# Fetching the global query and key rows of a windowed attention by indirect gathers, and giving batch 1 the schedule of the later batches

## The chip, the cores and the metric

The kernel runs on one core of a Trainium2 chip. Its engines are TensorE (PE, with its weight loads shown apart as PEld), VectorE (DVE), ScalarE (ACT), GpSimd (POOL) and SyncE (SP, which only issues transfers). Sixteen DMA engines move data between the chip's memory and the core. The metric is device time in microseconds (us) for one execution, the median of several; lower is better.

## The reference

A windowed attention with global tokens is followed by a two-layer block with a sine activation. B = 8 batches, H = 8 heads, S = 576 positions, D = 64, and NG = 8 positions in `global_idx`, the same for all batches and heads.

```python
scores = scale * np.matmul(q, k.transpose(0, 1, 3, 2))
mask = np.abs(pos[:, None] - pos[None, :]) <= 32
mask = mask | is_global[:, None] | is_global[None, :]
attn = softmax(np.where(mask, scores, -1e9))
x = matmul(attn, v)            # to (B*S, H*D) = (4608, 512)
h = x @ w_in                   # 512 -> 2048
g = h + sin(alpha * h)**2 / alpha
out = g @ w_out                # 2048 -> 512, float32
```

So every position sees its neighbours within 32 and the eight global positions, and the eight global positions see everything.

## The kernel before, in words

**Layout.** Positions go in 12 blocks of 48. A block's keys are 112 neighbours (48 and 32 on each side) and 8 global keys, so 120 rows; its queries are its own 48 and the 8 global ones, 56 columns. `kTw[hp]` (hp is one of four pairs of heads) holds the transposed keys of the blocks, with the global keys in columns 112 to 119 (`KB` to `KB + NG`); `qT[hp]` holds the transposed queries with the global ones in columns 48 to 55. Both are overwritten for each batch. Eight blocks make a unit, six units a batch. For a unit, `stage_Q` computes scores (PE), their exponential (ACT) and a product with a 0/1 mask (DVE, L474); `stage_D` the sums by a matmul with ones and a reciprocal as exp(-ln) on ACT; `stage_V` the product with the values in `VW` (batch parity) and a scaling on DVE into `xT`. `stage_G` finishes the global queries with eight small POOL copies into `xT` (L549).

**Phases.** Phase 0 is attention of batch 0. Then come, nine times, `mm1(p)`, 16 slots of `x @ w_in` with the activation, and, from phase 1 on, attention of batch p with `mm2(p - 1)`, the product with `w_out`, as filling between its stages. The first slots of `mm2` need the first half of `w_out`, the later ones the second. Attention of batch p + 1 has its first two head pairs transposed inside `mm1(p)` (`stage_T`, L430). From batch 2 on, all batches run the same list of steps, a `step(j)` in `attention`, with counts of filling slots after each (L816). Phases 0 and 1 have orders of their own, written out by hand (L782 and L794), in which K, q stand for transposes of keys and queries, G (or k, p) for the one-hot products below, Q, D, V for the stages, F for a slot of filling.

**Global rows before.** Batches 0 and 1: `globals_hp` (L369) multiplies the key and query tiles with a one-hot matrix `OH` on PE, 12 matmuls each for keys and queries of a head pair, and ACT or DVE copy the result into `kTw` and `qT` (L382). In phase 0 this is done within the order, in phase 1 for two head pairs within `mm1(0)` and for two in the order of phase 1. Batches 2 to 7: SP reads the eight indices into registers and issues transfers with register offsets (L339, L345): eight of batch 0's values, then eight each for values, keys and queries of all batches, 64 rows of 256 bytes each. They land in a part of the second `H2b` buffer. Near the end of phase 1 DVE casts the keys and queries (L354), PE transposes them in eight matmuls (L360), DVE copies them to `GT` (L365), and POOL copies from `GT` into `kTw` and `qT`, two copies for each head pair (`globals_in`, L396 and L400), in the batch before they are needed.

**Masks before.** Units 0 to 2 of batch 0 are masked on DVE as elsewhere. In units 3 to 5 PE adds a bias instead: two matmuls (L457) put a large negative `BIAS` in the scores first.

**Queues.** POOL issues all loads that cast from float32 to bfloat16: keys and queries of batch 0 in four pairs of heads (L131), its values (L114, L115, L118), the shifted second copy of `VW` (L146, L147), both halves of `w_in`, the values, keys and queries of batch 1, then the first half of `w_out`; the eight copies of L549 follow, then the second half of `w_out` (L710), in this order. POOL's queue, like each engine's, is in order. POOL transfers use eight semaphores in turn, so each waits until the eighth before it has landed. SP issues the gathers, the shift of `VW` for later batches and the output.

Of the kernel before, what the change touches and what calls it, by code (L numbers as in the profile page):

```python
# [13 lines left out]
DT = mybir.dt  # L14
# [3 lines left out]
def kernel(  # L18
# [61 lines left out]
    GT = const.tile([P, 2, NHP, B, NG], BF, name="GT")  # L80
# [3 lines left out]
    gN = [  # L84
        H2[1][0 : NG * B, 2 * i : 2 * i + 2, :].rearrange("p a n -> p (a n)").bitcast(F32)
        for i in range(3)
    ]
    gB = [H2[1][0 : NG * B, 6 + i, :] for i in range(2)]
    OH = const.tile([P, NTW, NG], BF, name="OH")
# [61 lines left out]
    def global_v(b):  # L151
# [27 lines left out]
    T6 = setup.tile([P, NTW], F32, name="T6")  # L179
    nc.gpsimd.iota(  # L180
        T6[:], pattern=[[TW, NTW]], base=0, channel_multiplier=1,
        allow_small_or_imprecise_dtypes=True,
    )
    kq0 = kq_loads(0, PAIRS)
    v0 = v_loads(0, ((0, H),))
    for f in kq0[:4]:
        f()
# [14 lines left out]
    zero_v(0)  # L202
# [3 lines left out]
    for f in v0 + kq0[4:]:  # L206
        f()
    Kps0 = psA0.tile([P, 2 * CH], BF, name="o2")

    def edges(t_):  # L210
# [5 lines left out]
    Vg32 = setup.tile([P, DM], F32, name="Vg32")  # L216
    zero(Vg32[96:128])
# [15 lines left out]
    Gf = setup.tile([P, NG], F32, name="Gf")  # L233
    nc.vector.tensor_copy(out=Gf[:], in_=gall[:].bitcast(DT.int32)[:, 0::2])
    nc.vector.tensor_tensor(
        out=OH[:], in0=T6[:, :, None].to_broadcast([P, NTW, NG]),
        in1=Gf[:, None, :].to_broadcast([P, NTW, NG]), op=ALU.is_equal,
# [38 lines left out]
    BIAS = setup.tile([P, NW + NB // 2, QC], BF, name="BIAS")  # L276
# [29 lines left out]
    def bias():  # L306
        nc.vector.tensor_scalar(
            out=BIAS[:], in0=MASK[:], scalar1=1.0, scalar2=-NEG, op0=ALU.subtract, op1=ALU.mult
        )

# [10 lines left out]
    VgZ = VgX[96:128, :, 0, :]  # L321

    def globals_v0():
        nc.vector.tensor_copy(out=VgZ, in_=Vg32[96:128].rearrange("p (h d) -> p h d", d=D))

    def globals_vn():
        G = VgX[0 : NG * B]
        nc.scalar.copy(out=G[:, :, 0, :], in_=gN[2].rearrange("p (h d) -> p h d", d=D))
        nc.scalar.copy(
            out=G[:, :, 1:, :], in_=G[:, :, 0:1, :].to_broadcast([NG * B, H, NU - 1, D])  # L330
        )

    def gather_all():
# [4 lines left out]
        for j in range(NG):  # L338
            nc.sync.dma_start(  # L339
                out=Vg32[KB + j : KB + j + 1, :].rearrange("p (h d) -> p h d", d=D),  # L340
                in_=v[0, :, bass.ds(regs[j], 1), :].rearrange("h o d -> o h d"),
            )

        def gather(i, src, j):
            nc.sync.dma_start(  # L345
                out=gN[i][j : NG * B : NG, :].rearrange("b (h d) -> b h d", d=D),
                in_=src[:, :, bass.ds(regs[j], 1), :].rearrange("b h o d -> b h (o d)"),
            )

        return [partial(gather, i, src, j) for i, src in ((2, v), (0, k), (1, q)) for j in range(NG)]  # L350

    def globals_cast():
        for i in range(2):
            nc.vector.tensor_copy(out=gB[i], in_=gN[i])  # L354

    def globals_all(pool, tag):
        gps = pool.tile([P, 2, NHP, NG * B], BF, name=tag)
        for i in range(2):
            for hp in range(NHP):
                nc.tensor.transpose(  # L360
                    out=gps[:, i, hp, :],
                    in_=gB[i][:, hp * P : (hp + 1) * P],
                    identity=identb[0 : NG * B, 0 : NG * B],
                )
        nc.vector.tensor_copy(  # L365
            out=GT[:].rearrange("p i h b g -> p i h (b g)"), in_=gps[:]
        )

    def globals_hp(b, hp, pool, tag, copy=nc.vector.tensor_copy, which=(0, 1)):  # L369
        gp = pool.tile([P, 2, NG], F32, name=tag)  # L370
        for i in which:
            src = qk[b][1 - i]
            for j in range(NTW):
                for t, pr in heads:
                    nc.tensor.matmul(
                        out=gp[pr, i, :],
                        lhsT=src[:, 2 * hp + t, j, :], rhs=OH[0:TW, j, :],
                        start=(j == 0), stop=(j == NTW - 1), skip_group_check=True,
                    )
        for i in which:  # L380
            dst = (kTw[hp][:, :, KB : KB + NG], qT[hp][:, :, QB:QC])[i]
            copy(  # L382
                out=dst, in_=gp[:, i, None, :].to_broadcast([P, NW, NG])
            )
# [10 lines left out]
    def globals_in(b, hp, eng=nc.gpsimd):  # L395
        eng.tensor_copy(  # L396
            out=kTw[hp][:, :, KB : KB + NG],
            in_=GT[:, 0, hp, b, None, :].to_broadcast([P, NW, NG]),
        )
        eng.tensor_copy(  # L400
            out=qT[hp][:, :, QB:QC],
            in_=GT[:, 1, hp, b, None, :].to_broadcast([P, NW, NG]),
# [27 lines left out]
    def stage_T(b, hp, pool, tag):  # L430
        T_K(b, hp, Kps, nc.vector.tensor_copy)
        T_Q(b, hp, pool, tag, nc.scalar.copy)
        if b == 1:
            globals_hp(b, hp, psC, "ops", nc.scalar.copy)
# [16 lines left out]
    def stage_Q(psA, b, n):  # L451
        Sp = psA.tile([P, 2, CH], F32, name="Sp")
        i0 = blocks(n)[0][1]
        biased = b == 0 and n >= NUN - NBIAS
        if biased:
            for t, pr in heads:
                nc.tensor.matmul(  # L457
# [13 lines left out]
        if biased:  # L471
            return E
# [275 lines left out]
    def start_sync():  # L748
        gathers.extend(gather_all())
        for f in gathers:  # L750
            f()
# [125 lines left out]
```

## Time and profile before

| What | Value |
|---|---|
| median of 10 runs | 380.0 us (376.95 to 383.35) |
| the profiled execution's own time | 381.6 us |
| its span, first to last instruction | 379.8 us |
| PE busy | 353.1 us, 93% of the span |
| ACT, DVE, POOL busy | 249.3, 233.6, 209.2 us |
| mean granted PE clock | 0.942 of full |
| phase 0 and `mm1(0)` | 0 to about 55.5 us |
| attention 1 with `mm2(0)` | 59.3 to 90.7 us |
| attention 2 with `mm2(1)` | 106.3 to 129.0 us |

The profile is of one execution, whose own time is 1.8 us above its span. A page gives the busy time of each engine, the span cut into 40 slices of 9.5 us with a digit for each engine's busy share in tenths, the clock that PE was granted in the same slices, the chain of work that ended last, and groups of instructions. A timeline lists instructions with start and duration, and in brackets how long the engine had been idle and what ended it. "Matmul busy" counts overlapping instructions, and small matmuls that follow one another are listed with a duration of about 0.2 us each although they start more closely.

### The profile page before, as it was taken

The page shows a single profiled execution, that of the slowest core. Times are in us where ns is not written, and L with a number is a line of the kernel's source. Part 1 is how long each engine was busy: PE and PEld are TensorE (multiplying, and loading weights), DVE is VectorE, ACT ScalarE, POOL GpSimd, SP SyncE. Part 2 cuts the span into 40 slices and gives each one's busy share as a digit, 9 for nine tenths or more (in the row PEclk, how much of TensorE's full clock was granted, in tenths as well). Part 3 has the DMA queues.
Part 4 walks back from the last instruction along what each step waited for, and adds up shares of the span by engine and source line. Part 5 has one row for each costly group of instructions (what it writes and reads, how often), then busy time and mean ns, then how long its engine had stood idle before and what let it go on. Part 6 is the DMA issues. An engine that isn't in the chain of part 4 may idle for free.

```text
span 379.8 us, 9614 instructions
## 1 busy us (share of the span) xinstructions
PE 353.1 (93%) x3832; PEld 175.9 (46%) x3832; DVE 233.6 (61%) x502; ACT 249.3 (66%) x381; POOL 209.2 (55%) x300
## 2 busy tenths in 40 slices
PE   6689986989999999999999999999999999999996
PEld 5444443444444444444544454444444444444444
DVE  6534583454876488648864886388638863866520
ACT  4547673465887588858885888588858884845411
POOL 9863496014893389338943894389438302965100
PEclk9555895799999999999999999999999999999999
DMA  9999999913199329942994279427933011000112
GB/s 80 167 196 173 188 173 165 99 57 100 35 65 179 110 41 58 176 109 49 58 173 113 51 52 168 115 59 50 173 101 71 2 42 73 0 2 28 55 58 83
DMA packets 132919, 35.55 MB, mean 94 GB/s; under 512 B 121674, under 2 KB 126698, under 8 KB 132874
## 3 DMA queue, kind: packets, MB, share of 16 engines
q0 software_dynamic: 121968, 19.91, 71.0%
q1 hardware_dynamic: 10602, 14.89, 14.0%
q8 instruction: 30, 0.49, 0.5%
q10 hardware_dynamic: 304, 0.14, 0.1%
q14 instruction: 15, 0.12, 0.1%
HBM read 38.95 MB, written 9.44 MB: 127 GB/s over the span
## 4 chain that ended last, share of the span: by engine, by line
PE 60%; ACT 14%; DVE 9%; DMA 6%; POOL 6%; issue 3%; POOLq 1%; ACTq 0%; DVEq 0%
PE hb L617 24%; PE ops L654 14%; PE o L654 11%; DMA w_out<-in_moe_w_out_dram 6%; ACT E L470 5%; PE num L515 3%; ACT Sb L624 3%; DVE kTw L417 2%; DVE S L632 2%; ACT L568 2%; PE Sp L464 2%; DVE H2b L607 2%; PE hb L654 2%; ACT rec L505 2%; ACT lnd L503 2%
## 5 line engine op out<-in xcount | busy, mean ns | idle before, releaser
L624 ACT ACTIVATE Sb<-hb,alphaT 128x512 bf16<-128x512 f32 x144 | 97.8, 686 | 57.3 <-PE hb L617 55.3
L617 PE MATMUL hb<-xT,w_in 128*128 128x512 bf16 x576 | 131.4, 382 | 1.3 <-DVE H2b L607 1.0
L632 POOL TENSOR_TENSOR S<-Sb 128x512 bf16<-128x512 bf16 x110 | 111.6, 1041 | 36.2 <-ACT Sb L624 36.2
L607 DVE SCALAR_TENSOR_TENSOR H2b<-S,recipT,hb 128x512 bf16<-128x512 bf16 x144 | 102.3, 740 | 25.7 <-POOL S L632 25.7
L617 PEld LDWEIGHTS <-w_in 128*128 128x128 bf16 x576 | 55.5, 98 | 69.0 <-issue 4.7
L654 PE MATMUL ops<-w_out,H2b 128*128 128x512 bf16 x304 | 76.9, 387 | 3.8 <-DMA w_out<-in_moe_w_out_dram 3.8
L654 PEld LDWEIGHTS <-H2b 128*128 128x128 bf16 x560 | 50.3, 99 | 62.1 <-issue 9.9
L470 ACT ACTIVATE E<-Sp 128x896 bf16<-128x896 f32 x48 | 43.5, 907 | 19.7 <-PE Sp L464 19.6
L654 PE MATMUL o<-w_out,H2b 128*128 128x512 bf16 x224 | 56.2, 390 | 0.0
L474 DVE TENSOR_TENSOR E<-E,MASK 128x896 bf16<-128x896 bf16 x45 | 28.3, 630 | 40.2 <-ACT E L470 40.2
L549 POOL COPY xT<-xg 128x4 bf16 x64 | 12.9, 201 | 61.0 <-DVE xg L547 57.4
L503 ACT ACTIVATE lnd<-den 128x384 f32<-128x384 f32 x48 | 23.5, 490 | 23.0 <-PE den L497 23.0
L533 DVE TENSOR_TENSOR xT<-num,rec 128x384 bf16<-128x384 f32 (+1 forms) x60 | 25.7, 449 | 12.5 <-PE num L515 9.8
L632 DVE TENSOR_TENSOR S<-Sb 128x512 bf16<-128x512 bf16 x26 | 18.2, 702 | 19.8 <-ACT Sb L624 19.6
L464 PE MATMUL Sp<-qT,kTw 64*128 64x56 bf16 x768 | 20.9, 192 | 8.5 <-ACT E L470 3.1
L464 PEld LDWEIGHTS <-kTw 64*128 64x128 bf16 x768 | 15.8, 97 | 23.9 <-issue 14.6
L515 PEld LDWEIGHTS <-VW 120*64 120x64 bf16 (+1 forms) x768 | 17.5, 117 | 19.3 <-issue 11.7
L505 ACT ACTIVATE rec<-lnd 128x384 f32<-128x384 f32 x48 | 25.1, 523 | 1.5
L417 DVE COPY kTw<-Kps 128x1344 bf16<-128x1344 bf16 x29 | 24.5, 846 | 1.0 <-PE Kps L408 1.0
L396 POOL COPY kTw<-GT 128x96 bf16<-128x96 bf16 x24 | 6.4, 269 | 32.6 <-PE num L515 20.5
L515 PE MATMUL num<-E,VW 120*64 120x56 bf16 (+1 forms) x720 | 20.4, 198 | 2.3 <-DVE gn L482 0.8
L131 POOL DMA_DIRECT2D KS<-in_k_dram x18 | 20.4, 1134 | 0.3 <-issue 0.3
(129 smaller groups left out, 305.5 us busy)
## 6 DMA issues: line engine op xcount, KB each, us to landing
out_dram<-osb SPq DMA_DIRECT2D x35, 256.0 KB
KS<-in_k_dram POOLq DMA_DIRECT2D x14, 288.0 KB, 8.3
QS<-in_q_dram POOLq DMA_DIRECT2D x14, 288.0 KB, 9.3
VW<-in_v_dram POOLq DMA_DIRECT2D x12, 336.0 KB, 11.2
VW<-VW SPq DMA_DIRECT2D x7, 384.0 KB
w_in<-in_moe_w_in_dram POOLq DMA_DIRECT2D x2, 1024.0 KB, 15.2
w_out<-in_moe_w_out_dram POOLq DMA_DIRECT2D x2, 1024.0 KB, 23.9
VW<-VW SPq DMA_DIRECT2D x7, 240.0 KB
```

The source lines that it names most:

```text
L417: copy(out=kTw[hp][:, :, 0:KB], in_=bass.AP(tensor=base.tensor, offset=base.offset, ap=[list(base.ap[0]), [QB, NW], [1, KB]],),)
L464: nc.tensor.matmul(out=Sp[:, t, m * QC : (m + 1) * QC], lhsT=kTw[hp][pr, i, :], rhs=qT[hp][pr, i, :], start=not biased, stop=True, skip_gr ...
L470: nc.scalar.activation(out=E[:], in_=Sp[:, :, 0:EW], func=AF.Exp, scale=scale)
L474: nc.vector.tensor_tensor(out=E[:], in0=E[:], in1=mk[:, None, :].to_broadcast([P, 2, EW]), op=ALU.mult)
L503: nc.scalar.activation(out=lnd[:], in_=den[:, :, 0:QB], func=AF.Ln)
L505: nc.scalar.activation(out=rec[:], in_=lnd[:], func=AF.Exp, scale=-1.0)
L515: nc.tensor.matmul(out=num[pr, m, :], lhsT=W[0:nk, i % 2, 2 * hp + t, i // 2, :], rhs=E[0:nk, t, m * QC : (m + 1) * QC], start=b > 0 or m ...
L607: nc.vector.scalar_tensor_tensor(out=H2b[:, n_, :], in0=s_[:], scalar=recipT[:, n_ : n_ + 1], in1=h_, op0=ALU.mult, op1=ALU.add,)
L617: nc.tensor.matmul(out=h2[:], lhsT=w_in[:, ci, nt * P : (nt + 1) * P], rhs=xT[:, ci, c * CH : (c + 1) * CH], start=(ci == 0), stop=(ci == ...
L624: nc.scalar.activation(out=Sb[:], in_=h2[:], func=AF.Sin, scale=alphaT[:, nt : nt + 1])
L632: eng.tensor_tensor(out=S2[:], in0=Sb[:], in1=Sb[:], op=ALU.mult)
L654: nc.tensor.matmul(out=ops[:], lhsT=H2b[:, nt, ts * P : (ts + 1) * P], rhs=w_out[:, nt, :], start=(nt == 0), stop=(nt == NT - 1),)
```

## The change

Four indirect transfers on POOL bring, for four batches at once, the global rows of all heads: `GKQ` has a row for each of (batch in the half, head pair, global index), 128 in all, for keys and queries and for the even and odd head of a pair. The row numbers `rowi` are computed on DVE from two small iotas and the indices. The first four are issued right after the first pair of key and query loads, so the rest of batch 0's loads stand behind them in POOL's queue; four more, for batches 4 to 7, are issued in phase 1 behind the loads of batch 2. `globals_t` transposes a half (four matmuls and one copy): the first half ("A") within phase 0, the second in phase 2. `globals_in` now serves all batches: for batch 0 on ACT and DVE (g0 to g3), for batch 1 on POOL (n0 to n3, in phase 0, behind the first half of `w_out` and ahead of the eight copies of `stage_G`).

With that go `globals_hp`, `OH`, the sixteen SP gathers of keys and queries and the eight of batch 0's values; batch 0's global values are taken from the gathered values of all batches by a small matmul with `SEL`. The bias matmuls go: units 3 to 5 of batch 0 get the DVE mask. Phase 1's own order goes: batch 1 runs the step list of the later batches. Cut to its core:

```diff
     kq0 = kq_loads(0, PAIRS)
     v0 = v_loads(0, ((0, H),))
-    for f in kq0[:4]:
+    for f in kq0[:2]:
         f()
...
+    rowi = const.tile([P, 1], DT.uint32, name="rowi")
+    nc.vector.scalar_tensor_tensor(
+        out=rowi[:], in0=I8[:, 0:1], scalar=float(2 * S), in1=Gsel[:, 0:1],
+        op0=ALU.mult, op1=ALU.add,
+    )
+    def gather_kq(i):
+        for kq, src in ((0, k), (1, q)):
+            for t in range(2):
+                nc.gpsimd.indirect_dma_start(
+                    out=GKQ[:, kq, i, t, :],
+                    out_offset=None,
+                    in_=src.rearrange("b h s d -> (b h s) d"),
+                    in_offset=bass.IndirectOffsetOnAxis(ap=rowi[:, 0:1], axis=0),
+                    element_offset=(i * 4 * H + t) * S * D,
+                )
+
     zero_v(0)
...
-    for f in v0 + kq0[4:]:
+    gather_kq(0)
+    for f in kq0[2:4] + v0 + kq0[4:]:
         f()
...
     def globals_v0():
-        nc.vector.tensor_copy(out=VgZ, in_=Vg32[96:128].rearrange("p (h d) -> p h d", d=D))
+        G = VgX[0 : NG * B]
+        nc.vector.tensor_copy(out=G[:, :, 0, :], in_=gN[:].rearrange("p (h d) -> p h d", d=D))
+        zp = psC.tile([P, DM], F32, name="ops")
+        nc.tensor.matmul(
+            out=zp[96:120, :], lhsT=SEL[:], rhs=G[0:NG, :, 0, :],
+            start=True, stop=True, skip_group_check=True,
+        )
+        nc.scalar.copy(out=VgX[96:120, :, 0, :], in_=zp[96:120, :].rearrange("p (h d) -> p h d", d=D))
...
+    def globals_t(i, pool, tag):
+        gps = pool.tile([P, 2, P], BF, name=tag)
+        for kq in range(2):
+            for t, pr in heads:
+                nc.tensor.transpose(out=gps[pr, kq, :], in_=GKQ[:, kq, i, t, :], identity=identb[:])
         nc.vector.tensor_copy(
-            out=GT[:].rearrange("p i h b g -> p i h (b g)"), in_=gps[:]
-        )
...
+            out=GT[:, :, i * B // 2 : (i + 1) * B // 2].rearrange("p i b h g -> p i (b h g)"), in_=gps[:]
+        )
...
-        if b == 1:
-            globals_hp(b, hp, psC, "ops", nc.scalar.copy)
...
-        biased = b == 0 and n >= NUN - NBIAS
-        if biased:
-            for t, pr in heads:
-                nc.tensor.matmul(
-                    out=Sp[:, t, 0:EW], lhsT=identb[:],
-                    rhs=BIAS[:, i0 : i0 + NB, :].rearrange("p u c -> p (u c)"),
-                    start=True, stop=False, skip_group_check=True,
-                )
...
-        go("warm sync K0 q0 G0 Q0 K1 k1 q1 p1 loads Q1 D0 Q2 D1 bias K2 k2 q2 p2 D2 Q3 K3 q3 D3 k3 p3 vg V0 Q4 V1 D4 Q5 V2 "
-           "V3 D5 V4 alpha V5 last keep vn wo")
...
-        go("L " * len(ld) + "F F Q0 Q1 K2 q2 G2 F F Q2 D0 K3 q3 G3 F D1 Q3 V0 F D2 Q4 V1 F F D3 Q5 gc V2 "
-           "F F D4 all V3 F D5 V4 F V5 g0 g1 g2 g3 last F F F F")
...
+        order = (
+            "warm K0 q0 A g0 Q0 K1 q1 g1 loads Q1 D0 Q2 D1 n0 n1 K2 q2 g2 D2 Q3 vg K3 q3 g3 D3 Q4 V0 V1 D4 Q5 n2 n3 V2 V3 D5 V4 "
+            "alpha V5 last keep vn wo"
+        )
...
+                parts, last = attention(p, psA, {2: -2, 3: 0})
+                counts = [1, 1, 1, 1, 1, 2, 2, 1, 0]
+                fill.pop(0)()
+                fill.pop(0)()
+                if p + 1 < B:
+                    with_extra(parts, load_slots(p + 1), 0, 4)
+                    if p == 1:
+                        parts[4] = partial(chain, parts[4], partial(gather_kq, 1))
+                    if p == 2:
+                        parts[4] = partial(chain, parts[4], partial(globals_t, 1, psA, "qp"))
```

## The prediction, made before the changed kernel was run

> **What bounds the kernel now.** I read the slices first, to find where PE is not the limit.
>
> ```profile
> PE   6689986989999999999999999999999999999996
> ...
> PEclk9555895799999999999999999999999999999999
> DMA  9999999913199329942994279427933011000112
> ```
>
> From slice 8 on (76 us) PE is busy nine tenths at full clock, and nothing in the change shortens that part. The first eight slices are different: the DMA engines are full, PE is not, and its clock is half for long. So the change is decided before 91 us. The windows, cut by phase, say what that front costs:
>
> ```profile
> core 0: us, PE busy (x) PEld busy (x) DVE busy (x) ACT busy (x) POOL busy (x), PEclk, DMA share, GB/s
> ...
> 59.20:71.00 11.80, 10.72 (x118) 5.28 (x120) 2.35 (x5) 2.83 (x4) 3.88 (x4) 0.50 2.17 158
> 71.00:90.70 19.70, 17.45 (x260) 8.90 (x257) 10.83 (x35) 11.89 (x20) 3.33 (x16) 1.00 0.35 57
> ...
> 106.30:129.70 23.40, 22.62 (x321) 11.15 (x320) 15.19 (x39) 16.93 (x27) 12.60 (x24) 1.00 1.37 117
> ```
>
> Attention 1 takes 31.4 us (59.3 to 90.7); attention 2, with the same stages and the same 16 filling slots, 23.4. Of the 8.0 us between them the first 11.8 run at clock 0.50. Then the chain that ended last, in order of time:
>
> ```profile
> 29.63 5.01 issue
> 34.66 24.48 DMA w_out<-in_moe_w_out_dram
> 59.14 0.14 issue
> 59.27 1.87 PE ops L654 x4
> ```
>
> Attention 1 starts when the first half of `w_out` lands; by the PE timeline PE had been idle 3.75 us for it, since 55.5, and that idle is what leaves the clock at half. Ahead of this half in POOL's queue stands everything the front loads. The timeline gives its issue times:
>
> ```profile
> 1.46 1.04 POOL L131 DMA_DIRECT2D KS<-in_k_dram  x1 [0.26 <-issue]
> ...
> 3.36 0.87 POOL L131 DMA_DIRECT2D KS<-in_k_dram  x1
> ...
> 5.67 1.56 POOL L114 DMA_DIRECT2D VW<-in_v_dram  x1
> ...
> 8.16 0.54 POOL L118 DMA_DIRECT2D VW<-in_v_dram  x1
> ...
> 35.77 2.04 POOL L549 COPY xT<-xg 128x4 bf16 x8 [0.23 <-DVE xg L547]
> ...
> 37.86 12.54 PE L617 MATMUL hb<-xT,w_in 128*128 128x512 bf16 x52 [0.29 <-POOL xT L549]
> ```
>
> Cut by the microsecond, the transfer view counts 1000 to 1230 short packets (128 bytes) per us from 4 us on, with a dip to 720 at 8; batch 0's 14,700 are through at 17.0. From 9 us on the DMA engines never wait for POOL.
>
> **Part 1, four gathers ahead of the queue (a cost).** They can start when `rowi` is ready: the cast of the indices (L234) ran at 3.35, four small DVE operations of 0.16 to 0.22 follow, so 4.2; POOL gets there at the same time (QS issued by 3.4, one more iota of 0.1, the large iota 0.64). So the wait itself costs nothing. What one gather costs on POOL, no row shows. Floor: L118, also 128 runs, 0.54. Ceiling: 2.0, the dearest direct form (L112, 5376 runs). By count of runs it is nearest to L118, but its addresses are looked up and not stepped, so I double that and a bit: 1.2, four 4.8. A gain is excluded, since the issue is added. KS of pair 1 then goes out at 9.0 in place of 3.36. The DMA engines have run dry by then (2304 runs of pair 0 and 512 of the gathers are two to three us of work). As with the first load, whose first packets came 1.5 us after its issue began, pair 1 flows from 10.5; 12,400 runs at 1,200 per us last 10.3, so batch 0 is through at 20.8 in place of 17.0: the whole stream is 3.8 late (ends 1.1 and 7.0). The large iota that moves ahead of them gives back the dip at 8 us; that is in the sum.
>
> [...] The row: POOL's first transfer took 1.04 against 0.87 for the next of its kind, so 0.2 at most for a first call here. [...]
>
> **Part 2, SP gathers leave the full stretch (a gain).** Of the 24 large SP gathers (64 runs each) the 16 of keys and queries vanish, and the eight of values come before 13 us, when the DMA engines are short of work; the eight small ones vanish too. In 20 to 40 us:
>
> ```profile
> q0 software_dynamic: 9981, 3.31, 148.6%
> q1 hardware_dynamic: 1169, 0.27, 11.2%
> ```
>
> 1169 packets were 11.2 of 160 shares, so 1.4 of the 20 us; all 1536 come to 1.8. That is an average over 16 engines. The engines are out of step: the first 1 KB packets of `w_out` appear at 42 us while short packets of the loads before it last until 53. [...] I take 2.8 (ends 1.8 and 4.5). So `w_out` lands at 59.1 + 3.8 - 2.8 = 60.1.
>
> **Part 3, phase 0.** One-hot products vanish (96 matmuls in phase 0) and six bias matmuls of 0.57 mean; three DVE masks of 0.63 come in. Phase 0 waits for data: K2 at 16.1 and q3 at 20.6 wait for DMA and move by 3.8, the shifted `VW` lands at 27 in place of 23.4, and the values stages follow it in some 8.5 us, to 35.5. POOL ends later. Its `w_out` issue at 34.66 came 0.3 after `w_in` had landed (34.3); that landing moves by 3.8 less two thirds of 2.8, to 36.2. Issue 0.9, then n0 to n3, eight copies at the pace of the eight at 83.5 (1.7), then the eight copies of L549 (2.0): `mm1(0)` starts at 41.2 in place of 37.9. That is work put ahead of L549 on POOL, and PE waits for it. The clock came up at 40.3 before, 5.9 us after PE's unbroken work began with the keep-warm matmuls; now a gap breaks that run, and some 3.6 us more of `mm1(0)` go at half clock, 1.8. The one-hot products inside it go: 0.49 and 0.51. So it lasts 17.65 + 1.8 - 1.0 = 18.4, to 59.6. Before, PE then stood idle until 59.3; that idle covers nearly all of this lateness, and what decides is again `w_out`, at 60.1.
>
> **Part 4, attention 1 (the gain).** It starts at 60.2, 0.9 late, after an idle of 0.6 instead of 3.75. Then it is the batch that lasts 23.4. Gone: one-hot products of two pairs (0.8 and 0.5), the two casts and eight transposes around 82 us (1.4), and the bare 1.0 of the hand-written order ahead of its second unit. [...] In the trace an idle of 3.75 did halve it, but it came back only at 70.9, after 6.5 unbroken busy us (64.3 to 70.9). [...] With an idle of 0.6 it should not drop, but that 0.6 is uncertain by more than 3; of 0 and 2.9 I take 1.5. Attention 1 lasts 24.9, to 85.1 in place of 90.7: 5.6 early. The second half of `w_out` landed at 64.5 and moves to 65.5; the fifth filling slot wants it at 66.
>
> **Part 5, later.** Four more gathers on POOL in phase 1, 4.8 us, on an engine with 7.2 busy of 31 there; they stand ahead of the copies for batch 2 (needed 20 us later) and L549 (some 10 later). At nothing; without that cover at most 4.8. In phase 2 four transposes and a DVE copy: 0.4.
>
> **Sum.** +0.9 - 6.5 + 0.4 = -5.2. Of the profiled 381.6 that leaves 376.4; that execution was 1.6 above the median, so 374.8 for 380.0.
>
> As a formula, with T for the four gathers: T - 10.0 with that clock, T - 8.6 if it drops.
>
> **Rivals.**
> - Gathers as cheap as L118 (T 2.1): `w_out` lands at 57.4, `mm1(0)` ends at 57, no clock loss: 23.4 to 80.9. 9.4 gained, 370.6. For: same number of runs. Against: looked-up addresses.
> - Given back: the stream is late by 7 (T 8), or the SP gathers cost only their average and PE idles long enough to halve the clock. 61.1 + 0.1 + 26.3 is 87.5, a gain of 2.8 (377.2); with T 8 as well about +0.5 (380.5). About 379. For: DMA-bound front, added issue at its very start.
> [...]
>
> **Chances.** As argued 0.40; cheap 0.14; given back 0.23; slower 0.23. A measurement of this kernel tells about 0.5% from no change, 1.9 us. Faster: 0.40 + 0.14 + 0.09 of the third; same: its other 0.14; slower 0.23. The range: from 369.5, just below the cheap case (0.05 left out), to 382.0, which leaves out the greater half of the slow case (0.14).
>
> **What would show it.** Right: indirect transfers of 1.2 on POOL from 4.2 us; KS of pair 1 at 9; `mm1(0)` at 41; less than 2 us of PE idle before the first L654 successor, at 60; clock 1.0 soon after; attention 1 in 24 to 26. Wrong: gathers over 2.5, or a gap of several us at the first; `w_out` landing past 64; or PE waiting inside attention 1 for the second half of `w_out`.

## The result, and the profile after

The changed kernel takes 376.6 us (median of 15 runs, 374.2 to 377.9); the kernel before, in the 52 runs beside it, 379.8. The ratio is 0.9915, 95% interval 0.9896 to 0.9935, so 3.2 us are gained. The profiled execution took 377.0 us with a span of 375.3, against 381.6 and 379.8: some 4.5 us less. The two differences are not the same because the profiled execution of before lay 1.8 above its median and that of after only 0.4.

That the former lay so high goes with its clock. In its trace PE is recorded at half clock for 13.65 us from 57.3 us on, around the wait for `w_out`, and its mean granted clock is 0.942. Executions of that kernel differ in this. Leaving out runs more than 1.5% above the fastest, the five with a mean of 0.942 took 381.4 to 383.4 us, the 21 with 0.954 or 0.955 took 378.3 to 380.1. A us at half clock takes half a us from that mean, so the latter have, by estimate from these figures, about 10 us less of it. Their traces weren't kept, so where in the kernel isn't shown; but the attention 1 of before that is shown, with its 31.4 us, is then one of the long ones.

The first slices of the page after, which answer to those shown of before:

```profile
PE   5539897999999999999999999999999999999996
...
PEclk9999999999999999999999999999999999999999
DMA  5999999975099509950994099319932001000112
```

The first slice of DMA fell from 9 to 5, and the second and third of PE from 6 and 8 to 5 and 3: the front is slower. From slice 7 on (66 us, the first slice being 0) PE is at nine tenths; before, it was so from slice 9 (85 us), since slice 8 has an 8. PEclk reads 9 everywhere; that it cannot be taken at its word is shown with the PE timeline below.

The windows of the same stages after, cut at its own borders, the last as long as that shown of before (start and end; length; busy us and count by engine; granted clock, DMA share, GB/s):

```profile
core 0: us, PE busy (x) PEld busy (x) DVE busy (x) ACT busy (x) POOL busy (x), PEclk, DMA share, GB/s
0.00:43.30 43.30, 26.90 (x363) 16.89 (x364) 20.85 (x84) 21.14 (x30) 32.24 (x56) 1.00 1.47 138
43.30:61.70 18.40, 17.77 (x113) 8.01 (x113) 12.27 (x19) 11.88 (x18) 10.83 (x11) 1.00 1.71 182
61.70:71.00 9.30, 7.47 (x113) 3.63 (x112) 5.15 (x9) 6.15 (x9) 9.00 (x9) 1.00 1.88 138
71.00:86.00 15.00, 14.43 (x205) 7.13 (x204) 8.94 (x28) 10.99 (x19) 6.88 (x20) 1.00 1.22 120
...
101.60:125.00 23.40, 22.54 (x324) 11.20 (x323) 15.18 (x40) 17.01 (x27) 12.69 (x24) 1.00 1.37 117
```

Phase 0 lasts 43.3 us (before 37.9), `mm1(0)` with what it waits for 18.4 (before 21.4, of which 3.75 idle), attention 1 24.3 (before 31.4). So 5.4 are lost, 3.0 come back in `mm1(0)` and 7.1 in attention 1: 4.7 less at the end of attention 1 (86.0 against 90.7), and after that the two kernels run side by side. Attention 2 ends at 124.45 against 129.0.

The chain that ended last, after:

```profile
9.64 0.98 POOL KS L126
...
14.54 0.79 POOL KS L126
15.33 7.68 DMA QS<-in_q_dram
...
35.63 0.63 DVE E L452
38.96 0.62 issue
43.34 12.03 PE hb L594 x44
...
63.10 1.33 DVE H2b L584 x2
64.47 1.02 PE o L631 x4
```

The landing of `w_out`, 24.5 us of the chain before, is gone from it. In its place the chain runs through POOL's queue behind the gathers, through the third pair of loads, attention 0, and then all of `mm1(0)`. POOL's timeline shows how the front comes about:

```profile
2.55 0.89 POOL L126 DMA_DIRECT2D QS<-in_q_dram  x1
3.44 0.64 POOL L182 IOTA IQ<- 128x576 f32 x1
4.41 1.05 POOL L221 DMA_INDIRECT GKQ<-in_k_dram,rowi  x1 [0.33 <-DVE rowi L214]
5.77 0.98 POOL L221 DMA_INDIRECT GKQ<-in_k_dram,rowi  x1 [0.30 <-issue]
7.05 1.07 POOL L221 DMA_INDIRECT GKQ<-in_q_dram,rowi  x1 [0.30 <-DMA GKQ<-in_k_dram,rowi]
8.43 1.21 POOL L221 DMA_INDIRECT GKQ<-in_q_dram,rowi  x1 [0.30 <-issue]
9.64 0.99 POOL L126 DMA_DIRECT2D KS<-in_k_dram  x1
...
14.46 0.96 POOL L126 DMA_DIRECT2D KS<-in_k_dram  x1
...
38.66 0.89 POOL L687 DMA_DIRECT2D w_out<-in_moe_w_out_dram  x1 [2.89 <-PE ops L329]
39.60 0.26 POOL L386 COPY kTw<-GT 128x96 bf16<-128x96 bf16 x1
...
41.27 2.02 POOL L527 COPY xT<-xg 128x4 bf16 x8
```

A gather takes 0.98 to 1.21 us with 0.3 between two: from 4.41 to 9.64 POOL does nothing else, 5.2 us. The first is no dearer than the others. The wait put down to L329 ahead of `w_out` is more likely for `w_in`, which landed at 38.3: before, too, `w_out` was issued 0.4 after that landing (34.3 and 34.66), and with a later `w_in`, in a run below, the issue moves along.

And the PE timeline:

```profile
5.20 0.69 PE L398 MATMUL Kps<-identb,KS 96*64 96x96 bf16 x12
...
21.77 0.69 PE L398 MATMUL Kps<-identb,KS 96*64 96x96 bf16 x12 [2.90 <-DMA KS<-in_k_dram]
...
43.34 13.74 PE L594 MATMUL hb<-xT,w_in 128*128 128x512 bf16 x52 [0.95 <-POOL xT L527]
57.01 0.45 PE L398 MATMUL Kps<-identb,KS 96*64 96x96 bf16 x12
...
61.69 1.03 PE L631 MATMUL ops<-w_out,H2b 128*128 128x512 bf16 x4
64.47 1.02 PE L631 MATMUL o<-w_out,H2b 128*128 128x512 bf16 x4 [1.75 <-DVE H2b L584]
```

The 12 transposes of L398 take 0.69 us in the front and 0.45 at 57 us, as the same ones did before at granted clock 0.50 and 1.00. So the front went at half clock, whatever the row of the clock says; by the spacing of the matmuls of L594 (0.43 us each, later 0.22) it came up at 48.0, inside `mm1(0)`. The trace explains the row: its first entry for the clock is this rise, at 48.1, and for the time ahead of it there is none. At 61.7 attention 1 begins with no wait for `w_out` at all; a wait of 1.75 us for L584, which ends `mm1(0)` on DVE, follows in front of the second filling slot.

### The profile page after: what moved, and what is told of

It reads as the page before. It is cut to its first block, busy times and chain, and to the rows that moved or that the text cites. A ratio compares the mean times of both kernels' runs of the same rounds, so it can differ in the third digit from the quotient of the medians.

```text
span 375.3 us, 9153 instructions
## 1 busy us (share of the span) xinstructions
PE 345.3 (92%) x3635; PEld 170.8 (46%) x3635; DVE 233.3 (62%) x502; ACT 249.2 (66%) x378; POOL 219.9 (59%) x317
## 4 chain that ended last, share of the span: by engine, by line
PE 64%; ACT 15%; DVE 12%; DMA 3%; POOL 3%; issue 1%; POOLq 0%; ACTq 0%; DVEq 0%
PE hb L594 28%; PE ops L631 14%; PE o L631 11%; ACT E L450 5%; DVE kTw L407 3%; PE num L493 3%; DVE S L609 3%; DVE H2b L584 3%; ACT Sb L601 3%; ACT rec L483 2%; ACT L545 2%; DMA QS<-in_q_dram 2%; PE Sp L444 2%; PE hb L631 2%; ACT lnd L481 2%; PE Kps L398 2%
## 5 line engine op out<-in xcount | busy, mean ns | idle before, releaser
L609 POOL TENSOR_TENSOR S<-Sb 128x512 bf16<-128x512 bf16 x110 | 111.6, 1041 | 40.4 <-ACT Sb L601 40.4
L594 PE MATMUL hb<-xT,w_in 128*128 128x512 bf16 x576 | 132.6, 384 | 2.3 <-DVE H2b L584 1.3
L584 DVE SCALAR_TENSOR_TENSOR H2b<-S,recipT,hb 128x512 bf16<-128x512 bf16 x144 | 102.3, 740 | 25.5 <-POOL S L609 25.5
L594 PEld LDWEIGHTS <-w_in 128*128 128x128 bf16 x576 | 55.8, 99 | 70.8 <-issue 6.9
L631 PE MATMUL ops<-w_out,H2b 128*128 128x512 bf16 x304 | 75.2, 380 | 0.0
L631 PE MATMUL o<-w_out,H2b 128*128 128x512 bf16 x224 | 54.4, 381 | 1.7 <-DVE H2b L584 1.7
L452 DVE TENSOR_TENSOR E<-E,MASK 128x896 bf16<-128x896 bf16 x48 | 30.5, 636 | 37.4 <-ACT E L450 37.4
L481 ACT ACTIVATE lnd<-den 128x384 f32<-128x384 f32 x48 | 23.5, 490 | 22.1 <-PE den L475 22.1
L444 PEld LDWEIGHTS <-kTw 64*128 64x128 bf16 x768 | 15.9, 96 | 22.4 <-issue 12.9
L126 POOL DMA_DIRECT2D QS<-in_q_dram x18 | 20.3, 1126 | 0.0
## 6 DMA issues: line engine op xcount, KB each, us to landing
VW<-in_v_dram POOLq DMA_DIRECT2D x12, 336.0 KB, 10.5
w_out<-in_moe_w_out_dram POOLq DMA_DIRECT2D x2, 1024.0 KB, 22.7
```

The source lines that it names most:

```text
L126: nc.gpsimd.dma_start(out=dst[:, h0 : h0 + nh].rearrange("p h t d -> p (h t) d"), in_=heads_ap(src, b, h0, 0, TW, 0, nh * NTW),)
L444: nc.tensor.matmul(out=Sp[:, t, m * QC : (m + 1) * QC], lhsT=kTw[hp][pr, i, :], rhs=qT[hp][pr, i, :], start=True, stop=True, skip_group_ch ...
L481: nc.scalar.activation(out=lnd[:], in_=den[:, :, 0:QB], func=AF.Ln)
L584: nc.vector.scalar_tensor_tensor(out=H2b[:, n_, :], in0=s_[:], scalar=recipT[:, n_ : n_ + 1], in1=h_, op0=ALU.mult, op1=ALU.add,)
L594: nc.tensor.matmul(out=h2[:], lhsT=w_in[:, ci, nt * P : (nt + 1) * P], rhs=xT[:, ci, c * CH : (c + 1) * CH], start=(ci == 0), stop=(ci == ...
L609: eng.tensor_tensor(out=S2[:], in0=Sb[:], in1=Sb[:], op=ALU.mult)
```

## The experiments

The theory after the result: the change is the sum of four parts that hardly touch one another, the step list for batch 1 (gain), the SP gathers that vanish (gain), the early gathers (loss), and the masks and one-hot products (little). The rival was that the gain hangs together: the list gains only because PE no longer idles for `w_out` and so keeps its clock. Each kernel is timed against the kernel before on its own chip, and ratios are to that. Differences in us are worked out from the ratios, on 379.8 us; the bare medians, partly from different chips, give others by up to about 1 us, and where that matters both are given.

**The early gathers alone.** Four unused gathers in the kernel before, at the place of the change:

```diff
+    gather_kq(0)
-    for f in v0 + kq0[4:]:
+    for f in kq0[2:4] + v0 + kq0[4:]:
         f()
```

> The kernel before with the four indirect gathers added at the place of the change, and nothing else; what they bring is not used. Theory T: they hold POOL for 5.2 us, the load stream is 5 to 6 us late as after the change, w_out lands 5 to 6 later (nothing relieves the queue), attention 1 starts that much later, and the kernel is 4.5 to 6.5 us slower. Rival R (the issue hides behind full DMA queues and costs little): slower by less than 2 us.

Measured: 385.9 us, ratio 1.0146 (1.0094 to 1.0199), 5.5 us slower. `mm1(0)` starts at 44.1 (before 37.9). And from the other side, the changed kernel without its first four gathers:

```diff
     zero_v(0)
-    gather_kq(0)
+    zero(GKQ[:, :, 0].bitcast(F32))
```

> The changed kernel without the first four gathers: the global keys and queries of batches 0 to 3 are left at zero, so its output is not the reference's; all else stays. Theory T: the load stream comes 5 to 6 us earlier, mm1(0) starts at 37.5 to 38.5 in place of 43.3, w_out lands at 56 to 57, attention 1 starts some 5 us earlier, and the kernel gains a further 4 to 5.5 us on the changed one (8 to 9 on the one before). Rival R: less than 2 us.

Measured: 372.7 us, ratio 0.9791 (0.9745 to 0.9836), 4.7 less than the changed kernel (3.9 by the medians). `mm1(0)` starts at 39.4 in place of 43.3, and attention 1 at 57.9, now after a wait for `w_out`:

```profile
57.91 1.02 PE L631 MATMUL ops<-w_out,H2b 128*128 128x512 bf16 x4 [2.34 <-DMA w_out<-in_moe_w_out_dram]
```

So the gathers cost about what POOL was held, 4 to 5.5 us, and the changed kernel would be 8 us faster than before if they were free.

**The SP gathers.** The sixteen of keys and queries back in the changed kernel, their rows unused:

```diff
+    def gather_sp():
+        for i, src in ((0, k), (1, q)):
+            for j in range(NG):
+                nc.sync.dma_start(
+                    out=gD[i][j : NG * B : NG, :].rearrange("b (h d) -> b h d", d=D),
+                    in_=src[:, :, bass.ds(dregs[j], 1), :].rearrange("b h o d -> b h (o d)"),
+                )
```

> The changed kernel with the sixteen SP gathers of keys and queries put back (into the same unused buffer as before; nothing reads them). Theory T with the relief of the prediction: w_in lands 1.5 to 3 us later, mm1(0) starts that much later, and with it attention 1; the kernel is 1.5 to 3.5 us slower than the changed one. Rival (64 runs each are lost in 120,000): slower by less than 0.5 us.

Measured: 381.0 us, ratio 1.0004 (0.9975 to 1.0032), 3.4 more than the changed kernel, at the upper end of what was expected, and 4.4 by the medians, above it. `w_in` lands at 42.3 in place of 38.3, and what follows it on POOL and PE moves with it:

```profile
42.72 0.89 POOL L702 DMA_DIRECT2D w_out<-in_moe_w_out_dram  x1 [7.30 <-PE qp L517]
...
47.40 0.59 PE L609 MATMUL hb<-xT,w_in 128*128 128x512 bf16 x1 [2.47 <-POOL xT L542]
```

In 20 to 40 us these transfers are 9.7 of 160 shares, 1.2 us of 20; that is what the sixteen engines lose on average. The landing lost 4.0. Why it lost more than that average isn't shown: the traces don't tell the engines apart.

**The step list alone.** In the kernel before, with only what the list needs placed anew (casts, transposes and copies of the gathered rows, a bank for the one-hot products of two pairs):

```diff
-                if p == 1:
-                    fill = mm2(0, H2[0], ((psC, "ops"), (psA, "o2")) * 2)
-                    fill[:8] = [fill[4 * (i % 2) + i // 2] for i in range(8)]
-                    phase_1(psA, fill)
...
+                    if p == 1:
+                        parts[5] = partial(chain, parts[5], globals_cast, partial(globals_all, psA, "qp"))
```

> The kernel before with one part of the change alone: batch 1 runs the step list of the later batches (one-hot products, SP gathers and bias matmuls all stay; only the order of phase 1 is changed). Theory T (the gain of the change sits in attention 1, half of it because PE no longer idles for w_out and keeps its clock, and the late load stream gives part of it back): w_out is still waited for 3 to 4 us, the first filling slots run at half clock, attention 1 takes 27 to 29 us in place of 31.4, so the kernel gains 2.5 to 4.5 us. Rival R (the gain is the work removed from phase 0 and the gathers): no more than 1 us gained.

Measured: 381.2 us, ratio 0.9999 (0.9967 to 1.0031): no gain, a miss. But the edit had made a wait of its own. The PE timeline of this kernel:

```profile
78.22 0.68 PE L360 MATMUL qp<-identb,H2b 64*128 64x64 bf16 x8 [2.84 <-DVE H2b L354]
79.24 1.49 PE L654 MATMUL o<-w_out,H2b 128*128 128x512 bf16 x3 [0.33 <-issue]
80.52 1.79 PE L654 MATMUL ops<-w_out,H2b 128*128 128x512 bf16 x4
```

Casts and transposes stand in one step, so PE waits 2.84 us for the casts on DVE, and after it four matmuls of `mm2` take 1.79 in place of 1.04: the clock had dropped (granted 0.91 over 71 to 90 us, so by estimate some 3.4 us at half). With the casts two steps earlier:

```diff
+                        parts[3] = partial(chain, parts[3], globals_cast)
-                        parts[5] = partial(chain, parts[5], globals_cast, partial(globals_all, psA, "qp"))
+                        parts[5] = partial(chain, parts[5], partial(globals_all, psA, "qp"))
```

> The kernel before with the step list for batch 1 alone, as in the first such run, but with the two casts of the gathered rows two steps ahead of their transposes, so that PE does not stand 2.8 us for them and lose its clock a second time (which that run did: it gained nothing). Theory T: w_out still waited for about 3 us, half clock until some 6 us after it, attention 1 in 27 to 28 us; 3 to 4 us gained on the kernel before. Rival R: the order of phase 1 is worth nothing, still no gain beyond 1 us.

Measured: 375.6 us, ratio 0.9899 (0.9867 to 0.9931), 3.8 less than before. The time is as expected, the length of attention 1 is not. The PE timeline:

```profile
59.65 1.86 PE L654 MATMUL ops<-w_out,H2b 128*128 128x512 bf16 x4 [4.55 <-DMA w_out<-in_moe_w_out_dram]
61.31 1.84 PE L654 MATMUL o<-w_out,H2b 128*128 128x512 bf16 x4
63.08 0.38 PE L464 MATMUL Sp<-qT,kTw 64*128 64x56 bf16 x16
63.39 1.04 PE L654 MATMUL ops<-w_out,H2b 128*128 128x512 bf16 x4
```

PE idles 4.55 us for `w_out`, longer than before, and begins at half clock (1.86 for four matmuls). Yet 3.4 us later it is at full clock, and attention 1 ends at 84.57, after 24.9 us (before 31.4, in a profiled execution with much half clock). The fair comparison is between executions with the same recorded clock. With 0.950 and 0.991 the list alone took 375.6 to 376.7 us (five runs), the kernel before 379.1 to 380.8 (fourteen). So the rival is out: the list has its gain with the idle, and at equal clock.

**The bias** back in units 3 to 5, in the changed kernel:

```diff
+        if biased:
+            for t, pr in heads:
+                nc.tensor.matmul(
+                    out=Sp[:, t, 0:EW], lhsT=identb[:],
+                    rhs=BIAS[:, i0 : i0 + NB, :].rearrange("p u c -> p (u c)"),
+                    start=True, stop=False, skip_group_check=True,
+                )
```

> The changed kernel with the bias matmuls of units 3 to 5 of batch 0 put back in place of the DVE mask. Theory T: phase 0 waits for its loads and ends on the POOL copies behind w_in's landing, so this moves the time by less than 1 us either way. Rival R (removed PE work is the gain): 2 to 3 us slower than the changed kernel, as six matmuls of 0.57 us mean come back.

Measured: 377.2 us, ratio 0.9931 (0.9905 to 0.9957). The interval overlaps that of the changed kernel: this part can't be told from nothing.

**The wait in front of the second slot.** The first two slots read the same tiles of `H2b`, so it isn't data that the second lacks. It opens the bank of `o`; the wait ends with an instruction of L584, which still reads banks of `mm1(0)`. The changed kernel with the filling slots in another order:

```diff
-                    fill[:8] = [fill[4 * (i % 2) + i // 2] for i in range(8)]
+                    fill[:8] = [fill[i] for i in (0, 1, 4, 5, 2, 6, 3, 7)]
```

> The changed kernel with the first filling slots of attention 1 in another order: two slots of the first output tile, then two of the second, where the changed kernel takes them in turn. All four need only the first half of w_out. In the changed kernel PE stands 1.75 us before the second slot, for the VectorE work that frees the bank of the second tile. If that wait is what it seems, it goes and the kernel gains 1 to 1.7 us; if the second half of w_out (landing near 66) is late for the fifth slot, the wait moves there and the gain is under 0.5 us.

Measured: 375.8 us, ratio 0.9896 (0.9860 to 0.9931), 0.7 less than the changed kernel, with overlapping intervals: neither expectation, and not told from nothing. A wait of 0.58 for `w_out` and one of 0.80 for L584 stand where the 1.75 was.

**Where the early gathers could go.** First behind all loads of batch 0, with all transposes ahead of the first scores, and with the new order of slots. The shift of batch 0's values also goes from POOL to SP, and the load of `moe_alpha` behind `w_in`:

```diff
-    gather_kq(0)
     for f in kq0[2:4] + v0 + kq0[4:]:
         f()
+    gather_kq(0)
...
-            "warm K0 q0 A g0 Q0 K1 q1 g1 loads Q1 D0 Q2 D1 n0 n1 K2 q2 g2 D2 Q3 vg K3 q3 g3 D3 Q4 V0 V1 D4 Q5 n2 n3 V2 V3 D5 V4 "
+            "warm loads K0 q0 K1 q1 K2 q2 K3 q3 A g0 Q0 g1 Q1 D0 g2 Q2 D1 n0 n1 g3 Q3 D2 vg D3 Q4 V0 V1 D4 Q5 n2 n3 V2 V3 D5 V4 "
```

> The changed kernel with the first four gathers behind all of batch 0's loads and directly ahead of w_in (all transposes of batch 0 come before the first scores, the shift of batch 0's values goes out on SP), and the slots as in the run with another order. Theory T: the DMA engines hold some 4.7 us of work when POOL comes to the gathers, so these cost the stream 1 to 2 us in place of 5 to 6; w_in lands near 34 to 35, mm1(0) starts at 38 to 40, and the kernel gains 4 to 6 us on the changed one (370 to 372.5). Rival: the first scores at 19 to 20 us in place of 12 make the attention itself the end of phase 0; then mm1(0) starts no earlier than 42 and the gain is under 2 us.

Measured: 380.0 us, ratio 0.9998 (0.9978 to 1.0019), 3.2 more than the changed kernel, a miss. Its PE timeline:

```profile
24.85 0.69 PE L397 MATMUL ops<-identb,QS 96*64 96x96 bf16 x12 [3.81 <-DMA QS<-in_q_dram]
25.34 0.56 PE L370 MATMUL num<-identb,GKQ 128*64 128x128 bf16 x4
26.75 0.56 PE L443 MATMUL Sp<-qT,kTw 64*128 64x56 bf16 x16 [0.86 <-ACT qT L389]
```

The loads now issue early, but nothing of attention 0 starts before the last pair has landed: first scores at 26.75 in place of 12.41. Attention 0 ends at 46.7 and `mm1(0)` starts at 49.1. `w_out` was issued at 35.0 (changed kernel 38.66); that was worth nothing. This run changed the place of the gathers and the order together, and the order decided.

Then behind the second pair only:

```diff
-    for f in kq0[:2]:
+    for f in kq0[:4]:
         f()
...
-    for f in kq0[2:4] + v0 + kq0[4:]:
+    for f in v0 + kq0[4:]:
         f()
```

> The changed kernel with the four early gathers behind the second pair of key and query loads in place of ahead of it. If the early gathers cost because the DMA engines run dry while they hold POOL (T), two loads more, 2300 short packets or two us of work, cover them: pair 1 of the keys goes out at 3.4 again, batch 0's loads are through near 21 in place of 22.8, mm1(0) starts 1.5 to 2 earlier, and the time is 374.0 to 375.5. If the cost is their work in the DMA engines themselves, or the hold on POOL whatever is queued ahead (rival), the time stays within 0.7 of the changed kernel's, 376 to 377.3.

Measured: 376.5 us, ratio 0.9888 (0.9840 to 0.9936): the changed kernel's median, with overlapping intervals. The rival is borne out, in its second form: the DMA engines stand idle meanwhile, so it is the hold on POOL and not the gathers' own work. The busy share of the DMA engines in 4 to 13 us, in 40 steps of 0.225 us, first of the changed kernel, then of this one:

```profile
DMA  9999999921630003610024611100391239999999
```

```profile
DMA  9999999999999999995311267001127310076011
```

With the second pair in front the DMA engines are full 2.3 us longer, and then run dry just the same. The hole has moved, not closed, since what follows in POOL's queue comes no earlier: the third pair's keys are issued at 14.28 (changed kernel 14.46, before 8.69), and their transposes can run at 22.1 (21.8, before 16.1). From issue to these transposes it is 7.3 to 7.8 us in all three.

**Without early gathers.** The last three kernels put the parts that gain together: the list, no SP gathers of keys and queries, and the eight indirect gathers in phase 1, where the front is over. Batches 0 and 1 keep one-hot products and bias. First all eight at the start of phase 1:

```diff
                 if p == 1:
+                    gather_kq(0)
+                    gather_kq(1)
...
+                        parts[5] = partial(chain, parts[5], partial(globals_t, 0, psA, "qp"), partial(globals_t, 1, psA, "qp"))
```

> The kernel before with the step list for batch 1 (casts two steps early is no longer needed), the sixteen SP gathers of keys and queries taken out, and all eight indirect gathers issued on POOL at the start of phase 1, where no load of the front stands behind them; batches 0 and 1 keep the one-hot products and the bias. T (the terms add: list -3.8, SP gathers' relief -4.4 as their return cost the changed kernel, early gathers 0): first half of the output weights lands at 55 to 56.5, mm1(0) starts near 35, the time is 370.5 to 373.0, ratio 0.975 to 0.981. Rival (the relief is only large when the gathers collide with the changed kernel's front, in the kernel before it is hidden in the wait for the output weights or is only the average 1.8): 374 to 376, landing at 57.5 or later. Slower rival (the eight gathers, 10 us of POOL at the start of phase 1, hold the copies that attention 1 needs): over 377, with PE waiting for POOL inside attention 1.

Measured: 376.8 us, ratio 0.9900 (0.9848 to 0.9952), no better than the list alone, a miss. The same with the other order of slots:

```diff
-                    fill[:8] = [fill[4 * (i % 2) + i // 2] for i in range(8)]
+                    fill[:8] = [fill[i] for i in (0, 1, 4, 5, 2, 6, 3, 7)]
```

> The same with the first eight filling slots of phase 1 in the order of use of their banks (0, 1, 4, 5, 2, 6, 3, 7). T: the wait of PE in front of the second slot (1.8 us in the changed kernel) goes, 0.5 to 1.0 less than the kernel without this order, so 369.5 to 372.5. Rival (the first slots want more of the second half of the output weights, or the wait moves behind them): within 0.5 of it.

Measured: 375.9 us, ratio 0.9874 (0.9829 to 0.9920), a miss too. The PE timeline of the first of the two shows why:

```profile
56.10 1.02 PE L679 MATMUL ops<-w_out,H2b 128*128 128x512 bf16 x4 [0.26 <-DMA w_out<-in_moe_w_out_dram]
...
73.81 0.30 PE L389 MATMUL qp<-identb,GKQ 128*64 128x128 bf16 x4 [2.48 <-DVE GT L390]
74.05 1.61 PE L679 MATMUL o<-w_out,H2b 128*128 128x512 bf16 x4
75.45 1.91 PE L679 MATMUL ops<-w_out,H2b 128*128 128x512 bf16 x4
```

Attention 1 starts at 56.1, 3.6 earlier than with the list alone: here is the relief. Then the second group of transposes waits 2.48 us until DVE has emptied the bank that both use, and the clock drops (1.91 for four in place of 1.04; granted 0.94 over attention 1, so by estimate some 3.5 us at half). It is the fault of the first kernel of the list again, in another place. The second group moved to phase 2, and its gathers behind batch 2's loads:

```diff
                     if p == 1:
-                        parts[5] = partial(chain, parts[5], partial(globals_t, 0, psA, "qp"), partial(globals_t, 1, psA, "qp"))
+                        parts[4] = partial(chain, parts[4], partial(gather_kq, 1))
+                        parts[5] = partial(chain, parts[5], partial(globals_t, 0, psA, "qp"))
+                    if p == 2:
+                        parts[4] = partial(chain, parts[4], partial(globals_t, 1, psA, "qp"))
```

> The kernel with all gathers late and the reordered filling slots, but only the first four gathers at the start of phase 1; the other four behind the loads of batch 2, and their four transposes in phase 2, as the changed kernel has them. T: in the two late-gather kernels PE stood 2.5 us because two groups of transposes share one bank, and some 1.5 us more went at half clock after it; that was the kernel's own doing and hid the relief of the SP gathers. Without it attention 1 runs from about 56.4 to 81.5 (25 us), 4.5 before the changed kernel, and the time is 371.0 to 373.0, ratio 0.975 to 0.982. Rival (the 2.5 us are absorbed by another wait, the masks on DVE or the exponentials on ACT, since attention 1 without a wait in front of it has not been seen under 24.3): 374 to 376.

Measured: 371.8 us, ratio 0.9769 (0.9722 to 0.9816), 8.8 us less than before and 5.5 less than the changed kernel (4.8 by the medians). Its PE timeline:

```profile
38.06 12.24 PE L642 MATMUL hb<-xT,w_in 128*128 128x512 bf16 x52 [0.30 <-POOL xT L574]
...
55.98 1.89 PE L679 MATMUL ops<-w_out,H2b 128*128 128x512 bf16 x8 [0.56 <-DMA w_out<-in_moe_w_out_dram]
...
80.11 4.26 PE L642 MATMUL hb<-xT,w_in 128*128 128x512 bf16 x19
```

`mm1(0)` starts as it did before the change, `w_out` lands 3.7 earlier than with the list alone (56.0 against 59.65), and attention 1 takes 24.1. The wait is gone, and four matmuls of `mm2` behind the first group take 1.04; but four gathers moved as well, so the wait and their place aren't told apart.

**The account.** The list gives 3.8 us. The SP gathers' absence gives 3.4 in the changed kernel (4.4 by the medians). In the kernel without early gathers, which also has the new order of slots, it gives some 5 beyond the list. The early gathers cost 5.5 when they are added to the kernel before, 4.7 when they are taken from the changed one (3.9 by the medians). The bias is within the noise. The one-hot products weren't run alone; without them and without early gathers the ratio is 0.9791, with them, without early gathers and with the new slots 0.9769, and the intervals overlap. The sum, list and SP gathers less early gathers, is a gain of 1.7 to 2.5 us by the ratios and of 4.3 with the figures in brackets; measured were 3.2. Single terms are good to 1 or 2 us, as the intervals say, so that the parts don't touch one another is borne out only to within that.

## Why the prediction was right, point by point

The predicted 374.8 is 1.8 below the 376.6, inside its range, and on the right side; of 5.2 us forecast, 3.2 came. In the profiled executions, for which the sum was made, 4.5 came. That is closer than its terms, which erred both ways, so the closeness is in part luck. And nearly all of the 1.8 is the 1.6 that was taken off to pass from that execution to the median: the profiled execution of after lay only 0.4 above its own. So far as the clock means tell, the excess was half clock, and no offset that stays: in the trace of after, PE is at full clock from 48.1 us to the end. One reading was off besides: slice 8 of before has an 8, so nine tenths begin at slice 9; nothing hangs on it.

- **Part 1, the gathers.** Estimated 4.8 from the nearest row, measured 5.2: a gather is as long as expected, and the 0.3 between two had been left out. The first call was no dearer: 1.05, and 0.98 to 1.21 for the others. But the stream is 6 late (batch 0's loads are through at 22.8), not 3.8. The first packets of the second pair came at 11.5 in place of 10.5, and then 12,400 runs took 11.3 us, some 1,100 per us in place of 1,200. The third pair's keys were simply issued 5.8 later and could be used 5.7 later, and the run with the second pair in front showed that a fuller start doesn't help them. This is the term furthest off.
- **Part 2, the SP gathers.** 2.8 was taken between 1.8 and 4.5; the 1.8 is worked out from the trace, what was put on top of it no run shows. The runs gave 4.0 at the landing of `w_in` and 3.7 at that of `w_out`: near the upper end. It made up for about half of the error of part 1: `w_out`, issued at 38.66, took 22.4 and landed near 61.1; the forecast had 60.1.
- **Part 3, phase 0.** `mm1(0)` was to start at 41.2 and started at 43.3. The failed step is that attention 0 would follow the shifted `VW` and end at 35.5, so that POOL decides; its last sums (`xg`) came at 40.4 (before 35.5), nearly as late as POOL, and of n0 to n3 only 0.9 showed. Its length, 18.4, was exact, but not by its terms: 2.2 us more at half clock (48.0 less 43.34, before 40.3 less 37.86) cost about 1.1 in place of 1.8, and a wait of 0.39 for DVE at 58.1 came in. So it ended at 61.7, and it, not `w_out`, decided when attention 1 starts. `w_out` was 0.6 ahead of it.
- **Part 4, attention 1.** 24.9 forecast, 24.3 measured; the end at 86.0 against 85.1. The mechanism was right in the main: the list of the later batches carries the gain. But the terms only happen to meet. The 23.4 for attention 2 is the length of the window; from its first slot to the next `mm1` it took 22.7 (106.31 to 128.97). The 1.5 for the clock, taken between 0 and 2.9, is a term that no run shows, and it wasn't called for: PE had not idled for `w_out`, and the first four matmuls took 1.03. In its place stood the wait of 1.75 for L584, which the sum does not have. The weight that the clock was given was too great: the list alone, after an idle of 4.55, still took only 24.9, with full clock 3.4 us after its first slot began. The 6.5 busy us that the trace before shows ahead of full clock need not be a property of the hand-written order: executions with that order differ in their clock, as said with the result. From the first slot on, half clock lasts 11.7 us in the kernel before (59.27 to 70.95), by estimate 5.6 in the first kernel of the list (granted 0.76 over 59.3 to 71.0) and 3.4 in the second (59.65 to 63.08). What decides between them wasn't isolated, and which piece of the list gives its 3.8 us wasn't either.
- **Part 5** cost nothing that shows: from the end of attention 1 the profiled spans are 289.3 and 289.1.
- **The rivals.** Gathers as cheap as L118 (0.54) did not come, nor the slower case: the four held POOL for 5.2 us, and no gather in any run took more than 1.32. Given back (about 379) was the nearest to what happened in the front: a stream 6 late, against 7 in that case; the SP gathers made up for most of it.

## What to carry to other kernels

In a front that one queue feeds, an instruction put at the head of the queue can cost all the time that it holds the queue; here that was so (5.2 us held, 4.7 to 5.5 lost), and two transfers put in front of it moved the hole without closing it. So gather what is needed late, late, and leave the first batches on what they have. Small transfers beside a full stream can delay the landing of a load by far more than their mean share of the engines: here 4.0 us against 1.2. When a reordering shows no gain, look for a wait of its own making (a bank used twice, a cast in the same step as its reader) before the idea is given up: here such a wait hid some 4 us or more in three kernels. And before a profiled stretch is taken for the rule, look at how the recorded clock differs from execution to execution.

## What the runs showed of the hardware that was not expected

- An indirect gather of 128 rows held POOL for 0.94 to 1.32 us and 0.3 more before the next, and landed 2.5 to 2.6 us after its issue in the changed kernel, where the DMA engines ran dry, but 9.2 to 12.5 behind batch 0's loads.
- The recorded clock of the changed kernel is 1.00 in the front, while transposes that take 0.45 at full clock take 0.69 there. The kernel with another order of slots, with the same front, has a 5 there from the second slice to the fifth (last line below). In this front the durations show the clock and the row does not.
- After the wait of PE for `w_out`, half clock lasted 11.7, some 5.6 and 3.4 us from the first slot on, after waits of 3.75, 3.05 and 4.55, in three traces (before, and the two kernels of the list). One kernel differs in its mean clock from one execution to the next: the kernel before took 378.3 to 380.1 us at a mean clock of 0.954 or 0.955, and 381.4 to 383.4 at 0.942.
- A PE wait of 2.5 to 2.8 us inside attention 1 was followed by about half clock for the next matmuls (1.79 and 1.91 for four in place of 1.04); after one of 1.75 us four took 1.02.
- Sixteen transfers of 64 rows, 1.2 us of DMA time by their share, put off the landing of a 1 MB load by 4 us.

```profile
PEclk9555599999999999999999999999999999999999
```
